# Seven operand tiles whose low halves move 128 bytes away from their high halves

## The chip, the cores and the metric

The kernel runs on one core of a Trainium2 chip. The metric is the time of one execution on the device, in microseconds (us). TensorE (PE in the profile) multiplies matrices, and its weight loads have a row of their own (PEld). VectorE (DVE), ScalarE (ACT) and GpSimd (POOL) do the elementwise work. SyncE (SP) issues every DMA. SBUF is the on-chip memory, PSUM the one that TensorE writes its sums to.

## The reference

A block-causal attention (4 batches, 8 heads, 576 positions, head size 64) gives 2304 rows of 512 values. Two layers follow, each of them two products with an elementwise function between them:

```
x = attention(q, k, v)                    # 2304 x 512
h = x @ w_in;   x = (h * cos(h)) @ w_out  # w_in 512 x 2048, w_out 2048 x 512
h = x @ w2_in;  x = relu(h)**2 @ w2_out   # the same sizes
```

All inputs and the output are float32.

## The kernel before, in words

**Precision.** A large product is computed from halves: an operand is split into a high part `hi`, rounded to the reduced type float32r that TensorE takes, and a low part `lo`, the rest. `mm3` (line 912 and on) makes three matmuls of each block: high by high, high by low, low by high.

**Stages.** Up to some 400 us the program interleaves attention with the first half (1024 of the 2048 inner columns) of the first layer. Three stages follow, and the change is about these. Stage 0 does the other half of the first layer, stage 1 one half of the second layer, stage 2 the other half. Each stage goes over the 2304 rows in five rounds, four of 512 rows and one of 256 (`ROUNDS`, in another order in each stage).

**Seven products.** In these stages `x @ w_in` is done on 2 by 2 blocks with seven block products in place of eight (`quad`; `two` for the round of 256 rows). This needs seven forms of x, which are blocks or sums of blocks: `load_quarters` makes them with four subtractions, and `x_parts` splits each into `hi` and `lo`, in one tile `x0` to `x6` of `[128, 2, 2, 256]`: two halves (`hi`, `lo`), two 128-row blocks of the inner dimension, 256 columns. There is one buffer of each tile, in the pool `x3`. A block product (`product`) is 12 matmuls `h<-x,w` of 128 by 128 weights (from a tile `w`, a form of the weight matrix) and 256 moving columns (from a tile `x0` to `x6`). In three stages these are 2304 matmuls: 3 x (4 rounds x 2 x 7 products + 1 round x 2 x 4 products) x 12.

**Keeping the forms.** Stage 1 and stage 2 need the same forms of x. `x_parts` writes the forms of the first four rounds of stage 1 to HBM (`xp_d<-x`, 24 DMAs of 512 KB), and `kept_parts` reads them back in rounds 2 to 5 of stage 2 (`x<-xp_d`, 24 DMAs). The first round of stage 2 uses what the last of stage 1 left in the tiles.

**Order.** A recording layer (`Recorder`) takes all operations, simulates their times with a table of costs and priorities, and writes out one order for all engines. `R.unit()` in `product` gives all 12 matmuls of a product one place in the priorities, so that they stand together.

**Addresses.** In the built program every `x0` to `x6` begins 320 bytes past a multiple of 512 in its partition, and its low half 2048 bytes further on, so also 320 past a multiple of 512. The weight tiles begin 384 past a multiple of 512 where they lie in the pool `wo` (first half of a round's products) and 256 past one in the pool `wa` (second half); the intermediate tiles `gh`, `gl` and `t` begin 64 past one. The two raw tiles `x` of the same pool, which stage 2 uses again for right-hand factors, begin 320 past one.

Of the kernel before, what the change touches and what calls it, by code (L numbers as in the profile page):

```python
# [2 lines left out]

# [8 lines left out]
F32R = mybir.dt.float32r  # L12
# [6 lines left out]
PSUM = bass.MemoryType.PSUM  # L19
# [37 lines left out]
class View:  # L57
    def __init__(self, vt, chain, ix, halves):
        self.vt, self.chain, self.ix, self.halves = vt, chain, ix, halves
# [34 lines left out]


class VTile(View):
    def __init__(self, pool, shape, dtype, tag, bufs, whole=False):
        self.pool, self.shape, self.dtype, self.tag, self.bufs = pool, shape, dtype, tag, bufs
        self.whole = whole
        n = int(np.prod(shape[1:]))  # L100
        self.grain = 32 if n >= 32 else 1
        self.full = (1 << (2 * (n // self.grain + 1))) - 1
        self.real = None
        self.users = []
        self.bank = self.banks = self.before = None
        super().__init__(self, [], np.arange(n).reshape(shape[1:]), 3)

    def alloc(self):
        if self.real is None:
            tag = self.tag if self.bank is None else f"bank{self.bank}"  # L110
            self.real = self.pool().tile(self.shape, self.dtype, tag=tag, name=self.tag, bufs=self.bufs)


class Banks:
# [30 lines left out]
class Recorder:  # L145
# [21 lines left out]
        self.phase = 0  # L167
        self.base = None

    def tile(self, pool, shape, dtype, tag, bufs=1, whole=False):  # L170
        return VTile(pool, shape, dtype, tag, bufs, whole)

    @contextmanager
    def of(self, kind):
# [207 lines left out]
def f(v):  # L382
    return v.bitcast(F32)


def real(v):
    return v.ap() if isinstance(v, View) else v
# [3 lines left out]
def kernel(  # L391
# [25 lines left out]
    R = Recorder()  # L417


    def of(kind):  # L420
        def wrap(fn):
            def run(*args, **kw):
                with R.of(kind):
                    return fn(*args, **kw)

            return run

        return wrap
# [40 lines left out]
    def hi_part(hi, x):  # L469
        n = hi.size  # L470
        flexible(
            "hi",
            {
                "POOL": (
                    "POOL", n * 0.836 + 160,
                    lambda: nc.gpsimd.tensor_scalar(real(hi), real(x), 1.0, 1.0, op0=ALU.mult, op1=ALU.mult),  # L476
                ),
                "DVE": (
                    "DVE", n / 1.92 + 68, lambda: nc.vector.tensor_scalar(real(hi), real(x), 1.0, None, op0=ALU.mult), 2,
                ),  # L480
                "ACT": ("ACT", n / 1.2 + 92, lambda: nc.scalar.activation(real(hi), real(x), ACTF.Copy)),  # L481
            },
            [hi], [x],
        )

    def lo_part(lo, x, hi):
        n = lo.size
        if psum(x):
            return tt(lo, x, f(hi), ALU.subtract)
        flexible(  # L490
            "lo",
            {
                "POOL": (
                    "POOL", n * 2.1 + 350,
                    lambda: nc.gpsimd.tensor_tensor(real(lo), real(x), real(f(hi)), op=ALU.subtract), 1,
                ),
                "DVE": (
                    "DVE", n / 0.96 + 68,
                    lambda: nc.vector.tensor_tensor(real(lo), real(x), real(f(hi)), op=ALU.subtract), 1,  # L499
                ),  # L500
            },
            [lo], [x, hi],
        )
# [76 lines left out]
    def dma(out, in_, size, service=None):  # L580
        R.op(
            "DMA", max(400.0, size / 360.0), lambda: nc.sync.dma_start(out=real(out), in_=real(in_)), [out], [in_],
            lat=1250,
        ).service = size / 420.0 if service is None else service
# [5 lines left out]
    class Pool:  # L590


        def __init__(self, name, **kw):
            self.name, self.kw, self.pool, self.after, self.stack = name, kw, None, (), None
# [18 lines left out]
    def later(names, **kw):  # L613
        return [Pool(n, **kw) for n in names]
# [32 lines left out]
    xs_p, tmp = opened(s1, "xs1", "tmp1")  # L647
    (sb,) = opened(att, "att", side="right")

    def T(pool, shape, dtype, tag, bufs=1):  # L650
        return R.tile(pool, shape, dtype, tag, bufs, whole=pool.kw.get("space") == PSUM)

    x_d = T(dram, [KD, 128, NT], F32, "x_d")
    y1_d = T(dram, [KD, 128, NT], F32, "y1_d")
    y_d = T(dram, [KD, 128, NT], F32, "y_d")


# [27 lines left out]
    for i in range(2):  # L685
# [3 lines left out]
        whole = T(sb, [128, 128], F32, f"whole{i}")  # L689
# [589 lines left out]
    for group, steps in WORK:  # L1279
# [6 lines left out]
        if group in ((0, 2), (1, 1)):  # L1286
            c = group[0]
            left_weights(w1_in, 2 + c, wi_d[c])
        if group in ((1, 2), (2, 1)):
            c = group[0] - 1  # L1290
            staged_weights(row_chunks(w1_out, 2 + c, 3 + c), wo_d[c:c + 1])
        if group == (3, 1):
            wo_p, x3_p = later(("wo", "x3"), side="right")
# [9 lines left out]
    def raw_rows(src, c0, n):  # L1303
# [5 lines left out]
            raw.append(t)  # L1309
        return raw  # L1310

    def x_tile(j):
        return T(x3_p, [128, 2, 2, 256], F32R, f"x{j}")

    def x_parts(forms, keep):

        ops = {}
        for j, x in forms:
            t = x_tile(j)
            hi, lo = t[:, 0], t[:, 1]  # L1320
            hi_part(hi, x)
            lo_part(lo, x, hi)
            if keep is not None:
                dma(keep[j], f(t).rearrange("p j k c -> p (j k c)"), 524288)
            ops[j] = hi, lo
        return ops

    @of("forms")
    def kept_parts(keep, which):

        ops = {}
        for j in which:
            t = x_tile(j)
            dma(f(t).rearrange("p j k c -> p (j k c)"), keep[j], 524288)
            ops[j] = t[:, 0], t[:, 1]
        return ops

    @of("forms")
    def load_plain(src, c0, keep=None):

        x1, x2 = raw_rows(src, c0, 256)
        d = T(tmp3, [128, 2, 256], F32, "t0")
        add(d, x2, x1, ALU.subtract)
        return x_parts(((0, x1), (1, x2), (4, d)), keep)

    @of("forms")
    def load_quarters(src, c0, keep=None):

        raw = raw_rows(src, c0, 512)
        b11, b12, b21, b22 = [t[:, :, o:o + 256] for t in raw for o in (0, 256)]  # L1350
        t1, t2, t3, t4 = [T(tmp3, [128, 2, 256], F32, f"t{i}") for i in range(4)]
        add(t1, b12, b11, ALU.subtract)
        add(t2, b22, t1, ALU.subtract)
        add(t3, b22, b12, ALU.subtract)
        add(t4, b21, t2, ALU.subtract)
        return x_parts(enumerate((b11, b21, b22, t4, t1, t2, t3)), keep)
# [195 lines left out]
    for stage in range(3):  # L1552
# [4 lines left out]
        for turn_, i in enumerate(ROUNDS[stage]):  # L1557
# [3 lines left out]
            if stage < 2:  # L1561
                xs = (load_quarters if i < 4 else load_plain)(src, c0, xp_d[i] if stage and turn_ < 4 else None)
                g = new_g()
            else:
                if turn_:
                    xs = kept_parts(xp_d[i], FIRST if i < 4 else (0, 1, 4))
                g = g_forms()
# [27 lines left out]
            if stage < 2 and 0 < turn_ < 3:  # L1595
                c = 2 * stage + turn_ - 1
# [62 lines left out]
```

## Time and profile before

| | us |
|---|---|
| median of 3 runs | 974.11 (973.11 to 974.89) |
| the profiled execution | 976.93 |
| its span, first to last instruction | 974.0 |
| PE busy in it | 953.0 (98%) |
| DVE, ACT, POOL busy | 695.7, 617.5, 204.0 |
| mean share of the TensorE clock granted | 0.989 |

The page gives each engine's busy time over the span. A matmul's duration in it covers the time in the pipeline, and matmuls overlap: one of 256 columns is shown with some 278 ns, while the next starts some 115 ns later. So the pace of a run of matmuls is read from the timeline, which merges a run of like instructions into one row with its start, its length and its count: the length less one duration, over the count less one, is the distance from start to start.

### The profile page before, as it was taken

The page shows a single profiled execution, that of the slowest core. Times are in us where ns is not written, and L with a number is a line of the kernel's source. Part 1 is how long each engine was busy: PE and PEld are TensorE (multiplying, and loading weights), DVE is VectorE, ACT ScalarE, POOL GpSimd, SP SyncE. Part 2 cuts the span into 40 slices and gives each one's busy share as a digit, 9 for nine tenths or more (in the row PEclk, how much of TensorE's full clock was granted, in tenths as well). Part 3 has the DMA queues.
Part 4 walks back from the last instruction along what each step waited for, and adds up shares of the span by engine and source line. Part 5 has one row for each costly group of instructions (what it writes and reads, how often), then busy time and mean ns, then how long its engine had stood idle before and what let it go on. Part 6 is the DMA issues. An engine that isn't in the chain of part 4 may idle for free.

```text
span 974.0 us, 19286 instructions
## 1 busy us (share of the span) xinstructions
PE 953.0 (98%) x6996; PEld 858.4 (88%) x6996; DVE 695.7 (71%) x1548; ACT 617.5 (63%) x1332; POOL 204.0 (21%) x299
## 2 busy tenths in 40 slices
PE   7879999999999999999999989999999999999998
PEld 5757987889897989998989879988998889999998
DVE  5998544675778455696879966997976737658565
ACT  6888688897878785574768655767664433324322
POOL 3223244588677771000000000000000000000000
PEclk8979999999999999999999999999999999999999
DMA  6754333455656449353355999897866779525321
GB/s 172 197 149 124 74 81 83 112 154 154 192 175 181 141 138 363 121 186 137 109 184 170 299 372 320 270 327 250 306 191 221 265 263 414 190 100 195 96 73 61
DMA packets 155150, 185.29 MB, mean 190 GB/s; under 512 B 71728, under 2 KB 119856, under 8 KB 155056
## 3 DMA queue, kind: packets, MB, share of 16 engines
q1 hardware_dynamic: 155056, 184.07, 57.9%
q8 instruction: 55, 0.90, 0.4%
q14 instruction: 39, 0.32, 0.1%
HBM read 114.29 MB, written 69.73 MB: 189 GB/s over the span
## 4 chain that ended last, share of the span: by engine, by line
PE 90%; DVE 5%; ACT 2%; DMA 1%; issue 1%; POOL 0%; POOLq 0%; DVEq 0%; ACTq 0%
PE y L557 39%; PE h L557 36%; PE t L575 6%; PE a L567 5%; PE s L567 4%; PE s L557 1%; DMA wi_d<-so 1%; DVE c L458 1%; DVE e L1059 1%; ACT e L442 1%; DMA x<-x_d 1%; DVE c L757 0%; DVE r L451 0%; DVE gl L499 0%; DVE w L499 0%
## 5 line engine op out<-in xcount | busy, mean ns | idle before, releaser
L557 PE MATMUL h<-x,w 128*128 128x256 f32 x2304 | 283.0, 278 | 0.2 <-ACT u L510 0.2
L557 PEld LDWEIGHTS h<-x,w 128*128 128x128 f32 x2304 | 278.3, 188 | 5.5 <-ACT u L510 0.3
L557 PE MATMUL y<-gh,w 128*128 128x256 f32 (+2 forms) x832 | 207.2, 329 | 8.2 <-POOL w L476 4.3
L557 PEld LDWEIGHTS y<-gh,w 128*128 128x128 f32 x832 | 142.8, 190 | 19.8 <-POOL w L476 4.8
L557 PE MATMUL y<-gl,w 128*128 128x256 f32 (+2 forms) x416 | 135.9, 329 | 0.0
L557 PE MATMUL y<-w,gh 128*128 128x512 f32 (+1 forms) x450 | 116.0, 353 | 0.4 <-DVE gh L499 0.4
L1059 DVE CUSTOM_DVE_ANT_0 e<-s,mask 128x288 f32<-128x288 f32 (+4 forms) x160 | 70.9, 479 | 32.8 <-PE s L567 26.2
L442 ACT ACTIVATE e<-e,st 128x256 f32<-128x256 f32 (+4 forms) x144 | 82.9, 577 | 5.9 <-DVE st L1059 3.8
L481 ACT ACTIVATE gh<-r 128x512 fp32r<-128x512 f32 (+1 forms) x101 | 58.2, 589 | 42.8 <-PE y L557 15.5
L540 POOL TENSOR_SCALAR e<-e,st 128x256 f32<-128x256 f32 (+4 forms) x120 | 73.2, 626 | 55.9 <-DVE st L1080 42.0
L557 PEld LDWEIGHTS y<-gl,w 128*128 128x128 f32 x416 | 79.1, 190 | 5.4 <-issue 0.5
L557 PEld LDWEIGHTS y<-w,gh 128*128 128x128 f32 x450 | 73.3, 188 | 11.4 <-DVE gh L499 0.6
L557 PE MATMUL y<-w,gl 128*128 128x256 f32 (+1 forms) x306 | 80.5, 332 | 0.0
L575 PE MATMUL t<-ident,e 128*128 128x128 f32 (+1 forms) x400 | 64.2, 283 | 3.8 <-DVE e L544 3.2
L557 PE MATMUL h<-xs2h,w 128*128 128x320 f32 x256 | 61.3, 313 | 0.0
L510 ACT ACTIVATE r<-t 128x384 f32<-128x384 f32 (+1 forms) x98 | 50.1, 534 | 15.2 <-PE t L575 14.5
L575 PEld LDWEIGHTS t<-ident,e 128*128 128x128 f32 (+1 forms) x400 | 46.6, 142 | 14.1 <-DVE e L544 4.7
L499 DVE TENSOR_TENSOR gl<-r,gh 128x512 fp32r<-128x512 f32 (+1 forms) x77 | 50.5, 670 | 7.8 <-ACT gh L481 7.0
L451 DVE TENSOR_TENSOR o<-y,o 128x512 f32<-128x512 f32 (+1 forms) x55 | 34.5, 634 | 27.9 <-PE y L557 26.3
L557 PEld LDWEIGHTS y<-w,gl 128*128 128x128 f32 x306 | 47.9, 188 | 6.1
L557 PE MATMUL h<-xs1h,w 128*128 128x256 f32 x256 | 51.0, 288 | 2.0 <-POOL w L476 1.1
L442 ACT ACTIVATE t<-raw,minus 128x512 int32<-128x512 int8 x64 | 48.8, 763 | 4.6 <-DMA raw<-in_moe_w_out_dram 2.6
(172 smaller groups left out, 1822.9 us busy)
## 6 DMA issues: line engine op xcount, KB each, us to landing
wi_d<-so SPq DMA_DIRECT2D x84, 256.0 KB, 3.2
w<-wi_d SPq DMA_DIRECT2D x42, 512.0 KB, 7.4
raw<-in_moe_w_in_dram SPq DMA_DIRECT2D x32, 512.0 KB, 4.8
raw<-in_moe_w_out_dram SPq DMA_DIRECT2D x32, 512.0 KB, 5.1
xp_d<-x SPq DMA_DIRECT2D x24, 512.0 KB, 6.8
x<-xp_d SPq DMA_DIRECT2D x24, 512.0 KB, 6.2
y_d<-o SPq DMA_DIRECT2D x34, 256.0 KB, 3.2
o<-y_d SPq DMA_DIRECT2D x32, 256.0 KB, 4.2
```

Of the source, the lines that this page charges most:

```text
L442: return nc.scalar.activation(real(out), real(in_), func, **kw)
L451: out.size / 0.96 + 68, lambda: nc.vector.tensor_tensor(real(out), real(a), real(b), op=op), [out], [a, b],
L458: lambda: nc.vector.scalar_tensor_tensor(real(out), real(a), s, real(b), op0=op0, op1=op1),
L481: "ACT": ("ACT", n / 1.2 + 92, lambda: nc.scalar.activation(real(hi), real(x), ACTF.Copy)),
L499: lambda: nc.vector.tensor_tensor(real(lo), real(x), real(f(hi)), op=ALU.subtract), 1,
L510: "ACT": ("ACT", n / 1.2 + 50, lambda: nc.scalar.activation(real(out), real(ps), ACTF.Copy)),
L540: lambda: nc.gpsimd.tensor_scalar(real(out), real(x), real(s), 1.0, op0=ALU.mult, op1=ALU.mult),
L557: lambda: nc.tensor.matmul(real(ps), lhsT=real(lhsT), rhs=real(rhs), start=start, stop=stop, skip_group_check=True),
L567: nc.tensor.matmul(real(ps), lhsT=real(l), rhs=real(r), start=start, stop=stop, skip_group_check=True)
L575: lambda: nc.tensor.transpose(real(out), real(in_), real(ident)[0:rows, 0:rows]), [out], [in_, ident],
L1059: lambda: nc.vector.tensor_tensor_reduce(out=real(e), in0=real(ps), in1=real(m), scale=-1.0, scalar=BIG, op0=ALU.add, op1=ALU.min, accum_o ...
```

## The change

The tiles `x0` to `x6` are allocated 32 elements (128 bytes) longer, as `[128, 1056]`, and a view on them is built whose step between the two halves is 544 elements in place of 512. The low half so begins 2176 bytes after the high half, where it began 2048 bytes after it. Within a half nothing changes. As the pool holds 7 x 128 bytes more and is filled from one fixed end, the tiles in it move too: `x3` by 128 bytes, the next by 256, and so on to `x0` and the two raw tiles `x` by 896. All of these are multiples of 128. After the change the high halves begin at 64, 192, 320 or 448 past a multiple of 512, and each low half 128 further round. The other pools stay.

The DMAs that keep the forms now have a gap on the side of SBUF, so their view there and in HBM is cut in two by halves: 2 KB runs in place of 4 KB runs, twice as many. Number, size, place and waits of the DMAs stay. No instruction of any engine moves.

```
 class VTile(View):
-    def __init__(self, pool, shape, dtype, tag, bufs, whole=False):
+    def __init__(self, pool, shape, dtype, tag, bufs, whole=False, apart=0):
...
+            if not self.apart:
+                self.real = self.pool().tile(self.shape, self.dtype, tag=tag, name=self.tag, bufs=self.bufs)
+                return
+
+            n, m = int(np.prod(self.shape[1:])), int(np.prod(self.shape[2:]))
+            t = self.pool().tile([self.shape[0], n + self.apart], self.dtype, tag=tag, name=self.tag, bufs=self.bufs)
+            a = t[:, 0:n].rearrange("p (a b c) -> p a b c", a=self.shape[1], b=self.shape[2])
+            self.real = dataclasses.replace(a, ap=[a.ap[0], [m + self.apart, self.shape[1]], *a.ap[2:]])
...
+    def by_half(t):
+        return t.rearrange("p (j c) -> p j c", j=2)
+
     def x_tile(j):
-        return T(x3_p, [128, 2, 2, 256], F32R, f"x{j}")
+        return T(x3_p, [128, 2, 2, 256], F32R, f"x{j}", 1, 32)
...
             if keep is not None:
-                dma(keep[j], f(t).rearrange("p j k c -> p (j k c)"), 524288)
+                dma(by_half(keep[j]), f(t).rearrange("p j k c -> p j (k c)"), 524288)
...
             t = x_tile(j)
-            dma(f(t).rearrange("p j k c -> p (j k c)"), keep[j], 524288)
+            dma(f(t).rearrange("p j k c -> p j (k c)"), by_half(keep[j]), 524288)
```

On SP's queue, the seven loads ahead of the second round of stage 2 stand like this in the kernel before (`xp_d` is the copy in HBM, the last column the shape of the transfer):

```order
L582 DMA x_10656<-xp_d_7857 128x1024
L582 DMA x_10667<-xp_d_7840 128x1024
L582 DMA x_10673<-xp_d_7600 128x1024
L582 DMA x_10686<-xp_d_7876 128x1024
L582 DMA x_10704<-xp_d_7617 128x1024
L582 DMA x_10721<-xp_d_7610 128x1024
L582 DMA x_10741<-xp_d_7814 128x1024
```

And like this in the changed one, at the same place of the queue:

```order
L590 DMA x_10656<-xp_d_7857 128x2x512
L590 DMA x_10667<-xp_d_7840 128x2x512
L590 DMA x_10673<-xp_d_7600 128x2x512
L590 DMA x_10686<-xp_d_7876 128x2x512
L590 DMA x_10704<-xp_d_7617 128x2x512
L590 DMA x_10721<-xp_d_7610 128x2x512
L590 DMA x_10741<-xp_d_7814 128x2x512
```

Their order is the same, and only the shape differs.

## Rows read from the trace of the kernel before

**Rows 1.** The page's first part: engine, busy us, share, instructions.

```profile
PE 953.0 (98%) x6996; PEld 858.4 (88%) x6996; DVE 695.7 (71%) x1548; ACT 617.5 (63%) x1332; POOL 204.0 (21%) x299
```

**Rows 2.** The page's chain that ended last, share of the span by engine.

```profile
PE 90%; DVE 5%; ACT 2%; DMA 1%; issue 1%; POOL 0%; POOLq 0%; DVEq 0%; ACTq 0%
```

**Rows 3.** Waits of PE from 400 us on: us in total, times, longest.

```profile
PE y L557 <- ACT gh L481: 2.7, 1, 2.7
PE y L557 <- DVE gh L499: 0.4, 1, 0.4
PE h L557 <- ACT u L510: 0.2, 1, 0.2
```

**Rows 4.** The page's costliest group: busy us, mean ns of one.

```profile
L557 PE MATMUL h<-x,w 128*128 128x256 f32 x2304 | 283.0, 278 | 0.2 <-ACT u L510 0.2
```

**Rows 5.** Timeline of PE, 793 to 811 us: start, length, engine, names, count.

```profile
792.81 14.33 PE L557 MATMUL h<-x,w 128*128 128x256 f32 x125
806.98 0.28 PE L557 MATMUL y<-raw,ws 128*128 128x256 f32 x1
807.10 4.17 PE L557 MATMUL h<-x,w 128*128 128x256 f32 x34
```

**Rows 6.** Tile h by stretches: length, busy PE, PEld, DVE, ACT, PEclk, DMA.

```profile
793.00:806.00 13.00, 13.00 (x117) 13.00 (x116) 2.76 (x4) 2.99 (x5) 1.00 0.89 318
838.00:849.00 11.00, 11.00 (x96) 11.00 (x94) 2.73 (x4) 2.40 (x4) 1.00 0.59 185
```

**Rows 7.** Groups of PE, 793 to 806 us, then 838 to 848 us.

```profile
L557 PE MATMUL h<-x,w 128*128 128x256 f32 x117 | 13.4, 276 | 0.0
...
L557 PE MATMUL h<-x,w 128*128 128x256 f32 x87 | 10.4, 280 | 0.0
```

**Rows 8.** Timeline of PE, 821 to 850 us.

```profile
822.47 1.57 PE L557 MATMUL h<-x,w 128*128 128x256 f32 x12
...
824.58 0.84 PE L557 MATMUL y<-w,gl 128*128 128x256 f32 x6
825.27 1.57 PE L557 MATMUL h<-x,w 128*128 128x256 f32 x12
...
837.12 0.84 PE L557 MATMUL y<-w,gh 128*128 128x256 f32 x6
837.80 11.47 PE L557 MATMUL h<-x,w 128*128 128x256 f32 x96
```

**Rows 9.** Timeline of PE, 597 to 600 us.

```profile
597.96 0.28 PE L557 MATMUL y<-gl,w 128*128 128x256 f32 x1
598.07 0.28 PE L557 MATMUL y<-gh,w 128*128 128x256 f32 x1
598.18 1.07 PE L557 MATMUL h<-x,w 128*128 128x256 f32 x8
```

**Rows 10.** Timeline of PE, 812 to 818.5 us.

```profile
816.17 0.88 PE L557 MATMUL y<-x,t 128*128 128x256 f32 x6
816.89 0.88 PE L557 MATMUL y<-x,gl 128*128 128x256 f32 x6
```

**Rows 11.** DMA issues: names, count, KB each, median us from issue to landing.

```profile
xp_d<-x SPq DMA_DIRECT2D x24, 512.0 KB, 6.8
x<-xp_d SPq DMA_DIRECT2D x24, 512.0 KB, 6.2
...
x<-x_d SPq DMA_DIRECT2D x8, 512.0 KB, 4.5
x<-y_d SPq DMA_DIRECT2D x8, 512.0 KB, 5.8
```

**Rows 12.** SP's issues of tile x: 812.0 to 812.4 us, then 812 to 820 us.

```profile
L582 SPq DMA_DIRECT2D x<-xp_d x1: 320/320/320, 812.1 to 812.1; - x1
DMA to landing us min/median/max: 9.9/9.9/9.9
...
L582 SPq DMA_DIRECT2D x<-xp_d x7: 319/319/320, 812.1 to 819.5; - x7
```

More of the change, by code (lines that the diff above doesn't have):

```diff
@@ L1 @@
+import dataclasses
 import heapq
@@ L96 @@
 class VTile(View):
-    def __init__(self, pool, shape, dtype, tag, bufs, whole=False):
+    def __init__(self, pool, shape, dtype, tag, bufs, whole=False, apart=0):
         self.pool, self.shape, self.dtype, self.tag, self.bufs = pool, shape, dtype, tag, bufs
-        self.whole = whole
+        self.whole, self.apart = whole, apart
         n = int(np.prod(shape[1:]))
@@ L110, in alloc @@
             tag = self.tag if self.bank is None else f"bank{self.bank}"
-            self.real = self.pool().tile(self.shape, self.dtype, tag=tag, name=self.tag, bufs=self.bufs)
+            if not self.apart:
[5 more added lines that the diff above has]
+            self.real = dataclasses.replace(a, ap=[a.ap[0], [m + self.apart, self.shape[1]], *a.ap[2:]])
 class Banks:
@@ L168, in __init__, with tile @@
         self.base = None
-    def tile(self, pool, shape, dtype, tag, bufs=1, whole=False):
-        return VTile(pool, shape, dtype, tag, bufs, whole)
+    def tile(self, pool, shape, dtype, tag, bufs=1, whole=False, apart=0):
+        return VTile(pool, shape, dtype, tag, bufs, whole, apart)
     @contextmanager
@@ L648, with T @@
     (sb,) = opened(att, "att", side="right")
-    def T(pool, shape, dtype, tag, bufs=1):
-        return R.tile(pool, shape, dtype, tag, bufs, whole=pool.kw.get("space") == PSUM)
+    def T(pool, shape, dtype, tag, bufs=1, apart=0):
+        return R.tile(pool, shape, dtype, tag, bufs, pool.kw.get("space") == PSUM, apart)
     x_d = T(dram, [KD, 128, NT], F32, "x_d")
```

## The prediction

> **What bounds the kernel now.** I read the page's first part and its chain first. PE is busy for 953.0 of 974.0 us [rows 1], and of the chain that ended last 90% is PE [rows 2]. Then the waits of PE from 400 us on, where the three stages that use the tiles lie: there are three waits, 3.3 us in all, and none ends with a DMA [rows 3]. The reader is to see in these that from 400 us on the time is the sum of the matmuls' distances from start to start. A change there counts only if it alters that distance, or makes a wait that isn't there now.
>
> Next I read the distance. The group that the change touches is `h<-x,w`, 2304 matmuls [rows 4]. The timeline shows two paces of it. From 792.81 us 125 of them take 14.33 us: less the last one's 0.28 that is 14.05 over 124 distances, 113.3 ns [rows 5]. From 837.80 us 96 take 11.47: 11.19 over 95, 117.8 ns [rows 8]. [...] The shown duration of one goes along, 276 ns at pace A and 280 at pace B [rows 7]. Over all 2304 the mean is 278 [rows 4], midway: about 1152 go at pace B. All at A would be 1152 x 4.5 ns = 5.2 us less than now, all at B 5.2 us more. There is a third pace in the trace, C: six `y<-x,gl` take 0.88 us, (0.88 - 0.28) / 5 = 120 ns [rows 10].
>
> **The change part by part.** It removes and adds no instruction and moves none. It changes addresses, and the shape of 48 DMAs.
>
> *Matmuls.* A third of the 2304, the 768 that stream a low half, now start 128 bytes further round in a cycle of 512 than those before and behind them; with the high halves these tiles move as a whole too, each by its own multiple of 128. What is that worth? The trace has no low half at another offset, so I look for places where an address takes such a step.
>
> - The weights take one. The stretch of 125 runs through the end of the first half of its round (weights at 384 past a multiple of 512) into the second half (256 past one), where the four last products of the run, 48 matmuls, lie. Were these at pace B, the mean would be (77 x 113.3 + 48 x 117.8) / 125 = 115.0 ns; it is 113.3 [rows 5]. The 96 at pace B cross the same step after 24 [rows 8].
> - The moving operand takes one, of 256 bytes. Up to 598.07 us `y<-gh,w` streams tiles at 64 past a multiple of 512, from 598.18 us on `h<-x,w` streams `x0` at 320. The starts are 597.96, 598.07 and 598.18: 110 ns apart to the row's resolution of 10, and the eight that follow take (1.07 - 0.28) / 7 = 113 ns [rows 9]. No step is seen.
> - The same addresses run at both paces. `x2` and `x3` with weights at 384 stand in the stretch at A (the last two products before the weights change) and again at the head of the one at B, a round later [rows 5, 8]. What differs is what ran before: the stretches at B follow `y` products. Behind the one `y<-raw,ws` at 806.98 us the pace is (4.17 - 0.28) / 33 = 117.9 ns, where it was 113.3 up to it [rows 5].
>
> So a pace is taken up at a switch between kinds of products and kept, and a step of 128 or 256 bytes in one of the operands changes neither. The places with C have moving operands and weights that both lie at an odd multiple of 64, while `h<-x,w` has the one at an odd, the other at an even multiple [rows 10, 5]. The change moves by multiples of 128, so it leaves odd odd. I therefore take 0 for the matmuls. Bounds, from the paces seen: -5.2 us (none left at B) and, at 120 ns for all 2304, 2304 x 120 - 2304 x (113.3 + 117.8) / 2 = +10.3 us.
>
> [...]
>
> *The 48 DMAs.* Each keeps its 512 KB and its place and is cut into twice as many runs of 2 KB. There are 512 KB loads in 2 KB runs already, `x<-x_d` and `x<-y_d`, with a median of 4.5 and 5.8 us to landing, against 6.2 and 6.8 of the 48 [rows 11]: shorter runs aren't seen to be slower, though these run beside other traffic. The cover is PE's own work, and it is thinnest ahead of the second round of stage 2. The seven loads there are issued from 812.1 to 819.5 us, 1.23 us apart, and the first lands 9.9 us after its issue, at 822.0 [rows 12]; the first matmul that needs it starts at 822.47 [rows 8]. That is some 0.5 us of slack; the second load (issued at about 813.4, landed by about 823.4) is needed at 825.27 [rows 8], 1.9 us of slack, and those behind it have more. Below, the cost is 0. Above, if every transfer took twice its 1.23 us, the first would come 1.23 - 0.5 = 0.7 us late and the second 2.5 - 1.9 = 0.6, which is the same wait and not another: 0.7 us once. I take 0, since the nearest rows are no slower. The 24 stores of stage 1 have nobody on PE behind them [rows 3].
>
> *Elementwise work* on the forms (ACT and DVE in stages 0 and 1) has the same instructions at other addresses; PE waits 0.2 us for ACT in all `h` products and not at all for DVE there [rows 3], which is the cover. If it were gone, a wait on ACT or DVE would stand ahead of `h` in the waits.
>
> **The sum.** Matmuls 0, DMAs 0, elementwise 0. The profiled execution took 976.93 us, span 974.0 and 2.9 around it, and stays there; the median of the runs, 974.11, lies 2.8 under it, and I forecast for the median 974.1 + 0 = 974.1. As paces are taken up at switches, a different moment of a few waits may hand out some anew: the rows show stretches of 12, 34, 96 and 125. With 38 matmuls in one, an estimate, there are some 60; if half of them changed, each by 38 x 4.5 ns = 0.17 us in either direction, that would be about 0.17 x square root of 30 = 0.9 us. This is within 1.95 us, the 0.2% that a measurement of this kernel can tell from no change.
>
> **Rivals.**
>
> *Faster: pace B needs the halves aligned.* A low half that no longer lies where the high half lies in the cycle of 512 would push a stretch at B out of its pattern, since two streams that met in each matmul no longer meet in the low ones. For it: one cause seems shared by all stretches at B, as they have the same distance of 117.8 ns in products of different tiles [rows 5, 8]. Against it: the weights' step of 128 bytes doesn't do that. Price: -5.2 us if all go, -2.6 if half go; 968.9 to 971.5, about 970.
>
> *Slower: pace A needs them.* Now each matmul's operand ends where, in the cycle of 512, the next one's begins, high or low; with the change the cycle jumps by 128 at the start of each low half and back behind it, 1536 jumps in the 2304. If fetching ahead across the jump costs what a switch costs, the stretches at A fall to B: 1152 x 4.5 = +5.2 us, 979.3; at 120 ns for all of them 984.4. For it: behind switches, where such jumps are, pace A is lost [rows 5, 8]. Against: at 598 us a jump of the moving operand isn't followed by a loss [rows 9]. It decides from one jump in three being paid for on: 512 x 4.5 = 2.3 us.
>
> *The change doesn't do what it says* is excluded for the addresses, which stand in the built program; that it does nothing to the time is the forecast itself. A wait on the first load (at most 0.7 us) lies within no change too.
>
> **How the numbers follow.** Forecast 0.62: the three steps without effect are the only direct evidence, but none is of a low half. Faster rival 0.21, slower 0.17: their prices are equal, and the pattern of B, kept only from a switch on, looks the easier one to break. Forecast's own range 972.5 to 975.8. The range to 8 in 10 leaves out a tenth on each side: half of the faster rival's 0.21 lies under 970, and half of the slower's 0.17 over 978, so 970 to 978. Faster by over 0.2% 0.21, within 0.62, slower 0.17.
>
> **What would show it.** Right: 276 to 280 ns with a mean near 278 for the 2304, 125 at A in one row near 793 us and 96 at B near 838 us, no DMA in the waits of PE. Faster: the stretch at 838 us at 113 ns, mean near 276. Slower: the stretch at 793 us at 118 ns or more, mean 280 or over. The step on the DMAs is wrong if `h` waits for `x<-xp_d` at 822 us by over 0.7 us. The forecast is wrong if the mean distance of `h<-x,w` moves by over 0.9 ns (2304 x 0.85 ns = 1.95 us).

## The result, and the profile after

The changed kernel takes 979.35 us (median of 6 runs, 978.46 to 981.2), the kernel before, on the same chip, 974.5 (973.09 to 976.18): ratio 1.0053, 95% interval 1.0037 to 1.0070, so 4.85 us slower. I had forecast 974.1. The price is that of the rival *Slower: pace A needs them*, 979.3.

The first part of the page of the changed kernel, then its row of the touched group (line 565 was 557):

```profile
PE 957.4 (98%) x6996; PEld 862.4 (88%) x6996; DVE 697.1 (71%) x1548; ACT 617.1 (63%) x1332; POOL 204.2 (21%) x299
```

```profile
L565 PE MATMUL h<-x,w 128*128 128x256 f32 x2304 | 287.7, 280 | 0.0
```

PE is busy 4.4 us longer than in [rows 1], with the same number of instructions; DVE and ACT differ by less than 1.5. The group `h<-x,w` is busy 287.7 us where it was 283.0 [rows 4]: 4.7 us, all that is to be explained. Divided by 2304 that is 2.0 ns more from one start to the next, and the mean shown duration, 278 before, is now the 280 of pace B, the one of 117.8 ns [rows 7, 8].

The waits of PE from 400 us on:

```profile
PE y L565 <- ACT gh L489: 0.8, 2, 0.5
PE y L565 <- DVE gh L507: 0.4, 1, 0.4
```

They come to 1.2 us, 2.1 less than in [rows 3]. So the two spans differ by only 4.7 - 2.1 = 2.6 us (976.6 and 974.0): the profiled execution of before holds one wait of 2.7 us for `gh`, and lies 2.4 us over the median of its own runs. No wait is on a DMA. The 48 transfers (names, KB, median us to landing) are 0.2 us quicker than in [rows 11]:

```profile
xp_d<-x SPq DMA_DIRECT2D x24, 512.0 KB, 6.6
x<-xp_d SPq DMA_DIRECT2D x24, 512.0 KB, 6.0
```

The timeline of PE where before the stretch of 125 stood at pace A, 113.3 ns [rows 5]:

```profile
793.53 15.67 PE L565 MATMUL h<-x,w 128*128 128x256 f32 x132
809.04 0.28 PE L565 MATMUL y<-raw,ws 128*128 128x256 f32 x1
809.16 3.11 PE L565 MATMUL h<-x,w 128*128 128x256 f32 x25
```

(15.67 - 0.28) / 131 = 117.5 ns, where it was 113.3. Tile h in two stretches of the changed kernel, as in [rows 6] (length, busy PE with count, granted clock, DMA):

```profile
794.00:807.00 13.00, 13.00 (x113) 1.00 0.92 323
840.20:851.20 11.00, 11.00 (x96) 1.00 0.56 169
```

In the first, 13 us now hold 113 matmuls, not 117; in the second 11 us hold 96 as they did. The granted clock is 1.00 in both, as it was in both of [rows 6], and PE is busy throughout: neither the clock nor a wait makes the difference. So what was at pace A lost it, and what was at pace B stayed. From the start times of all neighbours in the group (2201 distances in each trace, gaps left out) the mean goes from 115.6 to 117.6 ns, and 175 distances lie under 115 ns where 1107 did. The rest are no longer even: 112 to 123 ns, about a mean near that of B.

### The profile page after: what moved, and what is told of

Same layout as the page of the kernel before. It is cut to its first block, busy times and chain, and to the rows that moved or that the text cites. A ratio compares the mean times of both kernels' runs of the same rounds, so it can differ in the third digit from the quotient of the medians.

```text
span 976.6 us, 19286 instructions
## 1 busy us (share of the span) xinstructions
PE 957.4 (98%) x6996; PEld 862.4 (88%) x6996; DVE 697.1 (71%) x1548; ACT 617.1 (63%) x1332; POOL 204.2 (21%) x299
## 4 chain that ended last, share of the span: by engine, by line
PE 90%; DVE 4%; DMA 3%; ACT 2%; POOL 1%; issue 1%; SPq 0%; POOLq 0%; ACTq 0%; DVEq 0%
PE y L565 38%; PE h L565 37%; PE t L583 6%; PE a L575 5%; PE s L575 3%; DMA wi_d<-so 2%; PE s L565 1%; DMA raw<-in_moe_w_in_dram 1%; DVE c L466 1%; DVE c L765 0%; POOL e L548 0%; DVE e L1067 0%; ACT e L450 0%; DVE gl L507 0%; DVE r L459 0%
## 5 line engine op out<-in xcount | busy, mean ns | idle before, releaser
L565 PE MATMUL h<-x,w 128*128 128x256 f32 x2304 | 287.7, 280 | 0.0
L565 PEld LDWEIGHTS h<-x,w 128*128 128x128 f32 x2304 | 282.8, 188 | 5.3 <-ACT u L518 0.2
L565 PE MATMUL y<-w,gh 128*128 128x512 f32 (+1 forms) x450 | 116.1, 353 | 0.4 <-DVE gh L507 0.4
```

The source lines that it names most:

```text
L565: lambda: nc.tensor.matmul(real(ps), lhsT=real(lhsT), rhs=real(rhs), start=start, stop=stop, skip_group_check=True),
```

## The experiments

A remark on the rows: a window of 10 us counts the matmuls that reach into it, so its pace is (10.00 + 0.28) / count: 91 or 90 at pace A, 87 or 88 at B, 85 or 86 at C. "Mean distance" is worked out as above from the start times of the group.

**Jumps, own addresses, or the DMAs?** Three kernels put the seven forms into one block of SBUF, all high halves, a gap, all low halves, so that each address can be chosen; order and transfers stay, and a few waits of DVE are met one matmul earlier.

```diff
-            self.real = self.pool().tile(self.shape, self.dtype, tag=tag, name=self.tag, bufs=self.bufs)
...
+            h, l = HALVES[self.tag]
+            block = self.pool.block = self.pool.block or self.pool().tile([128, BLOCK], self.dtype, tag="block", ...)
+            a = block[:, h:h + 1024].rearrange("p (a b c) -> p a b c", a=2, b=2)
+            self.real = dataclasses.replace(a, ap=[a.ap[0], [l - h, 2], *a.ap[2:]])
```

`HALVES` gives the places of the two halves in 4-byte elements: `x0` stands at (0, 3712) for the gap of 512 bytes, (0, 3616) for 128, (0, 3648) for 256, and each further form 512 elements on.

> The kernel before with the seven x forms in one block of SBUF: all high halves in a row, then 512 bytes of nothing, then all low halves. Every half begins at 320 modulo 512, as in the kernel before; the form's DMAs go in two runs of 2 KB, as in the changed kernel. Theory 1 (pace A needs each 256-column matmul's moving operand to begin where the one before ended, modulo 512): no jump is left, so 974.5 us and the mean distance of the 2304 matmuls near 115.6 ns. Rival 2 (the forms' own start addresses modulo 512 decide): the same, 974.5. Rival 3 (the 2 KB runs of the DMAs cost the time): 979. Rival 4 (chance: any change of addresses draws the paces anew): anything from 970 to 979.

> The same block, but the low halves 128 bytes past a multiple of 512 behind the high ones: high halves all at 320 modulo 512, as before, low halves all at 448. Theory 1: 1536 of the 2304 matmuls begin 128 bytes away from where the one before ended, as in the changed kernel: 979.3 us, mean distance near 117.8 ns. Rival 2 (own addresses): only the 768 matmuls on low halves have a new address, a third of 5 us: 976. Rival 3 (2 KB runs): 979, as for the 512-byte gap. Rival 4: anything from 970 to 979.

> The same block with the low halves 256 bytes past a multiple of 512: high halves at 320 modulo 512, low halves at 64. Theory 1 with a period of 512 bytes: 1536 jumps again, 979. Theory 1 with a period of 256 bytes: no jump counts, 974.5. Rival 2: a third of the effect at most, 976. Rival 3: 979. Rival 4: anything from 970 to 979.

The fourth keeps the changed kernel's tiles but puts the low half directly behind the high one (32 elements of extra length, no gap, no offset), and its DMAs go in one run again:

```diff
...
-        return T(x3_p, [128, 2, 2, 256], F32R, f"x{j}", 1, 32)
+        return T(x3_p, [128, 2, 2, 256], F32R, f"x{j}", 1, (32, 0, 0))
...
```

> The seven forms' tiles are 128 bytes longer, as in the changed kernel, so each begins where it does there (64, 192, 320 or 448 modulo 512), but the low half follows the high half directly and the DMAs are one run of 4 KB, as before. Theory 1: no jump inside a product; only some 190 places where the form changes have one: if each costs only its own matmul, +0.4 us, 975; if a jump leaves pace A for the rest of its product of 12 matmuls, up to 979. Rival 2 (own addresses): 1944 of the 2304 matmuls have another address, 978.7. Rival 3 (2 KB runs): 974.5. Rival 4: anything from 970 to 979.

The group of h in the four, in the order gap 512, 128, 256, then tiles moved:

```profile
L569 PE MATMUL h<-block,w 128*128 128x256 f32 x2304 | 283.0, 278 | 0.2 <-ACT u L522 0.2
```

```profile
L569 PE MATMUL h<-block,w 128*128 128x256 f32 x2304 | 287.9, 280 | 1.8 <-ACT u L522 1.8
```

```profile
L569 PE MATMUL h<-block,w 128*128 128x256 f32 x2304 | 283.3, 278 | 0.8 <-ACT u L522 0.8
```

```profile
L566 PE MATMUL h<-x,w 128*128 128x256 f32 x2304 | 285.7, 279 | 0.0
```

| kernel | ratio to before (95%) | mean distance |
|---|---|---|
| gap 512 | 1.0001 (0.9990 to 1.0012) | 115.6 ns |
| gap 128 | 1.0040 (1.0022 to 1.0059) | 117.7 ns |
| gap 256 | 1.0000 (0.9987 to 1.0014) | 115.6 ns |
| tiles moved, no gap | 1.0025 (1.0013 to 1.0037) | 116.8 ns |

The gap of 512 has the changed kernel's DMA runs of 2 KB and costs nothing: rival 3 falls. The gap of 256 costs nothing either, and both repeat the paces of before nearly one by one (1108 and 1100 distances under 115 ns; 1107 before): rival 4, chance, falls, and 256 bytes count as no jump, so the cycle is 256 bytes and not 512. The gap of 128, with every high half where it was, brings the whole 4.9 us back in the group: rival 2 had a third. The moved tiles have no jump inside a product and only 95 jumps of 128 modulo 256 between products, and cost 2.7 us in the group. That is far more than 95 matmuls' worth: a jump's effect outlasts its own matmul. Lay the built program's addresses beside the start times of this trace, and the pace before and behind most of these jumps can be told. Where the distance from stationary to moving operand goes from 192 to 64 modulo 256, the pace is B behind it in 23 cases of 23, 15 of which came from A; where it goes from 64 to 192, it is A in 20 cases of the 26 that came from B, and B in all 4 that came from A. In 30 of the 95 the weights step by 128 together with the moving operand, so that the distance stays; there too A is lost, in all 6 cases that came from it. So a jump of the moving operand that meets pace A ends it whichever way the distance goes, and only a step of the distance from 64 to 192 mostly turns B to A.

**Fewer jumps at the same addresses.** Each product runs its eight matmuls on the high half first:

```diff
-                    mm3(ps[:, m], (w[i][:, 0, c], w[i][:, 1, c]), (hi[:, k], lo[:, k]), ...)
+                    for n in range(2):
+                        matmul(ps[:, m], w[i][:, n, c], hi[:, k], ...)
+            for m in range(2):
+                for k in range(2):
+                    ...
+                    matmul(ps[:, m], w[i][:, 0, c], lo[:, k], False, k == 1, holds)
```

> Control for the next kernel: forms as in the block with the 512-byte gap (no jump), but each product of 12 matmuls runs its eight matmuls on the high half first and its four on the low half last, where it was high, low, high by turns. The list of instructions comes out somewhat differently for this, so its time against the kernel before is open, 972 to 978; it is to be compared with the next one.

> The same order (eight matmuls on the high half, then four on the low half), the low halves 128 bytes past a multiple of 512: the same addresses as in the block with the 128-byte gap, which ran at 980.1, and the same share of matmuls on them, but only two jumps in 12 matmuls, 384 in all instead of 1536. Theory 1 (a jump between consecutive moving operands is what costs, and the pace comes back after it): a quarter to a half of 5 us above its control. Rival 2 (a low half 128 bytes off costs wherever it stands): the full 5 us above its control. Rival 5 (any jump throws the pace to B until the next gap): also nearly the full 5 us.

The order costs both a wait of 6.4 us on `w` elsewhere, so only the two are compared: 987.45 and 990.37 us, ratios 1.0126 (1.0108 to 1.0144) and 1.0150 (1.0133 to 1.0168). These intervals overlap, so the reading rests on the group rows, control first:

```profile
L569 PE MATMUL h<-block,w 128*128 128x256 f32 x2304 | 282.6, 278 | 2.7 <-DVE r L463 1.4
```

```profile
L569 PE MATMUL h<-block,w 128*128 128x256 f32 x2304 | 285.6, 280 | 0.7 <-ACT block L493 0.5
```

302 jumps (some of the 384 fall where other matmuls stand between) cost 3.0 us in the group, 1517 (gap 128) cost 4.9, 95 (tiles moved) cost 2.7. So my "a quarter to a half" of 5 us was too low and rival 5, nearly all of it, too high. The price grows far less than the count of jumps. An estimate of its bound is what was at pace A: 1107 distances, at 4.5 ns each 5.0 us.

**The place against the stationary operand.** The block 64 bytes on (both operands at even multiples of 64); everything 64 bytes on (moving even, stationary odd); jumps of 64:

```diff
-    shim(ctx, "shim1", 32)
+    shim(ctx, "shim1", 96)
-    shim(ctx, "shim3", 96, side="right")
+    shim(ctx, "shim3", 160, side="right")
```

That is the second. The others change only the block's table: `x0` at (16, 3728) for the first, (0, 3600) for the third.

> The block with the 512-byte gap, moved as a whole by 64 bytes: no jump inside or between products (all halves at 384 modulo 512), but the moving operands now begin at even multiples of 64, as the stationary ones do (256 and 384). Theory 1 with period 256 alone (only jumps count, the place does not): 975. Theory 6 (the place counts against the stationary operand's: both on even or both on odd multiples of 64 give pace C, as the trace of before has it for the matmuls of y on x and gl): all 2304 at 120 ns, (120 - 115.6) x 2304 = +10 us, 985.

> The kernel before with every tile of SBUF moved by 64 bytes (upwards on the left side, downwards on the right), nothing else: the forms begin at 256 modulo 512 and the weights of h at 320, which is how the matmuls of y on w and gh stand in the kernel before (256 and 64), and those always run at pace A there; y's own matmuls then stand as h's did. Theory 1 (only jumps count): 975. Theory 6 (place against the stationary operand): h all at pace A, (115.6 - 113.3) x 2304 = 5.3 us less, 970, from which y's 256-column matmuls may take back up to 2 us.

> One look: the block with the low halves 64 bytes past a multiple of 512 (high halves at 320 modulo 512, low halves at 384): 1536 jumps of 64 bytes, and the 768 matmuls on low halves stand on an even multiple of 64 as their weights do. Theory 1: at least as slow as the 128-byte gap, mean distance 117.7 ns or more, 980; with theory 6, 768 of them at 120 ns and more, up to 118.5 ns and 982. If a jump of 64 bytes counted for nothing: 115.6 ns, 975.

Group rows in that order:

```profile
L569 PE MATMUL h<-block,w 128*128 128x256 f32 x2304 | 290.8, 282 | 0.0
```

```profile
L557 PE MATMUL h<-x,w 128*128 128x256 f32 x2304 | 283.8, 279 | 0.7 <-DMA x<-xp_d 0.6
```

```profile
L569 PE MATMUL h<-block,w 128*128 128x256 f32 x2304 | 289.2, 281 | 0.1
```

With both on even multiples the ratio is 1.0069 (1.0056 to 1.0081), the mean distance 119.1 ns, and 1114 of the distances are 120: pace C, without one jump, as the prediction read it from [rows 10]; the expectation had 10 us by theory 6, and 7.8 came in the group. The 64-byte jumps (a single run, 980.32 us) cost 6.2 us in the group. The other half of theory 6 fell: with all places exchanged h was at B as often as before or a little more (1005 distances under 115 ns, mean 115.7), ratio 1.0015 (1.0005 to 1.0025). Its premise was not right either: the matmuls `y<-w,gh` of before don't always run at A, 107 of 148 of their distances lie under 115 ns.

**By itself.** Stretches of 96 matmuls on zeros in one accumulator, without waits, put in ahead of the kernel. Three kernels do this, and each ran once. The code is that of the second and third; the first steps only the moving operand:

```diff
...
+            for mov, stat, lo, wl in PARTS:
+                for i in range(96):
+                    o, w = mov + (lo if i % 3 == 1 else 0), stat + (wl if i % 3 == 2 else 0)
+                    nc.tensor.matmul(real(ps)[:, 0:256], lhsT=real(z)[:, w:w + 128], rhs=real(z)[:, o:o + 256], ...)
```

> The disputed cost by itself: the kernel before with nine stretches of 96 matmuls of 256 columns on zeros put in at its start, back to back in one accumulator, no waits between, the stationary operand always the same. In a stretch the middle one of each three reads its moving operand 0, 128, 256 or 512 bytes further on; the place is as h has it (moving on an odd multiple of 64, stationary on an even one), but for one stretch with both on odd ones. In order: 0, 0, 128, 0, 256, 128, 512, both odd 0, 0. The time of the whole kernel (about 100 us more) says nothing. Theory 1 with period 256: the two stretches with 128 at 117.5 ns and more from start to start; those with 0, 256 and 512 alike, at 113.3 or 117.8 as they fall; both odd: 120. Against it: all stretches alike, which would mean that the offset matters only beside changing weights and accumulators.

Windows of PE inside the stretches with steps of 128, 256, 128, then with both operands on odd multiples, then without steps:

```profile
32.00:42.00 10.00, 10.00 (x88) 1.00 0.36 119
...
54.50:64.50 10.00, 10.00 (x88) 1.00 0.31 109
65.50:75.50 10.00, 10.00 (x87) 1.00 0.01 2
...
88.00:98.00 10.00, 10.00 (x85) 1.00 0.00 0
100.00:110.00 10.00, 10.00 (x87) 1.00 0.01 2
```

All stand at B, 117.8 ns, jumps or none, and at 120 where both are odd. The four stretches not shown are at 117.8 too, by their start times. Jumps of 128 don't slow pace B on average (117.79 with them, 117.77 without). So they can cost only by what they do to pace A, and this run never had it.

> The separate measurement again, with ten stretches of 96 matmuls, to see what brings pace A about: without a jump the last such run stayed at 117.77 ns throughout, and in the kernel with h on even multiples pace B turned to pace A wherever the stationary operand's address stepped from 192 to 64 modulo 256. Now the third of each three reads its stationary operand 0, 128 or 256 bytes further on, the middle one its moving operand 0 or 128. Moving on odd and stationary on even multiples of 64: steps of the stationary operand 0, 128, 0; moving on even and stationary on odd ones: 0, 128, 0; then both operands with steps of 128, in either place; then a stationary step of 256 (odd moving); then none (even moving). Theory 7 (a 128-byte step of the stationary operand sets pace A, a 128-byte step of the moving one unsets it): the stretches with stationary steps alone at 113.3 ns, and those after them without steps stay at 113.3; with both steps 117.8. Theory 1 alone (only the moving operand's steps count, and they only keep pace A away): all stretches near 117.8.

Windows in the first, second and sixth stretch, then those with both operands stepping (two places), then the stationary step of 256:

```profile
9.00:19.00 10.00, 10.00 (x91) 1.00 0.58 168
20.00:30.00 10.00, 10.00 (x91) 1.00 0.52 159
...
64.00:74.00 10.00, 10.00 (x91) 1.00 0.01 2
75.00:85.00 10.00, 10.00 (x85) 1.00 0.00 0
86.00:96.00 10.00, 10.00 (x87) 1.00 0.00 0
97.50:107.50 10.00, 10.00 (x90) 1.00 0.01 2
```

This time the first stretch was at A already, with the same instructions and addresses as the first of the run before. So these alone don't set the pace. At the entry the two differ: the first two starts are 207 ns apart here and 200 in the run at B. Whether that decides isn't shown. Steps of the stationary operand by 128 leave A alone, as the prediction had read from [rows 5]; the moving operand's, with them, end it (120.8 ns in the first of the two places, 117.7 in the second). Whether stationary steps set A this run can't say.

> The separate measurement a third time, twelve stretches of 96 matmuls, since no stretch so far had steps of the moving operand alone and began at pace A. Moving on odd, stationary on even multiples of 64 and always the same. Steps of the middle moving operand in order: 0; 256; 0; then all 96 of a stretch 128 further on (one single step at its start); back again (one single step); 128 in every third; 0; then the stretch with both operands stepping by 128 on the other multiples, to shake the pace; 0; one single step of 128; 128 in every third; 0. Theory 1 (jumps of 128 keep pace A away): wherever pace A, 113.3 ns, is found, the stretch with 128 in every third leaves it for 117.8 on average or more, and the one without steps behind it stays at 117.8 or finds A again by chance; a step of 256 keeps A. A single step of 128: either A is lost for the whole stretch behind it (a jump throws the pace to B), or a few matmuls are slower and A comes back (a jump costs only its own matmuls). Against theory 1: 113.3 in the stretches with 128 in every third.

Windows in the stretches four to seven (all 128 on; back; 128 in every third; none), then nine to twelve (none; 128 on; 128 in every third; none):

```profile
43.00:53.00 10.00, 10.00 (x88) 1.00 0.50 176
54.50:64.50 10.00, 10.00 (x91) 1.00 0.32 108
65.50:75.50 10.00, 10.00 (x87) 1.00 0.01 2
76.50:86.50 10.00, 10.00 (x90) 1.00 0.00 0
...
99.00:109.00 10.00, 10.00 (x91) 1.00 0.01 2
110.00:120.00 10.00, 10.00 (x87) 1.00 0.01 2
121.00:131.00 10.00, 10.00 (x88) 1.00 0.00 0
132.00:142.00 10.00, 10.00 (x87) 1.00 0.00 0
```

The fifth stretch is at A, the sixth, with jumps of the moving operand alone, isn't; the seventh, without, is again. One single step of 128 behind the ninth puts the tenth to B for all of its 96, and it was one single step back that had put the fifth to A. No stretch in which jumps of 128 of the moving operand come again and again is at A, in any of the three runs; where they stop, the pace may be either.

**Can pace A be had?** Three tries, each with the order, semaphores and transfers of before. The first stands h's moving operand on even, its weights on odd multiples of 64 throughout, and leaves y as it is:

```diff
-            self.real = self.pool().tile(self.shape, self.dtype, tag=tag, name=self.tag, bufs=self.bufs)
...
+            o = 16 * (SLOTS[self.pool.slot] % 2 != self.odd)
...
+            t = self.pool().tile([128, 1040], self.dtype, ...)[:, o:o + 1024]
```

> An attempt at a faster kernel, from the traces so far: no jumps, and all 2304 matmuls of h with the moving operand at an even multiple of 64 bytes (256 modulo 512) and the stationary one at an odd multiple, as the matmuls of y on w stand in the kernel before and keep standing here. For this the wo and x3 pools lie 64 bytes lower, and the tiles of the wa pool are 64 bytes longer, with h's weights on odd and y's weights on even multiples. Order, waits and transfers are those of before. Theory 6 (place against the stationary operand decides between the paces): h at pace A but for the first few of each stretch, 2304 x (115.6 - 113.6) = 4.6 us less, 970.4; in the run with every tile moved by 64 bytes half of h stayed at B, so half of it, 972.5, is the other end. Theory 1 alone (only jumps count): 975.

```profile
L569 PE MATMUL h<-x,w 128*128 128x256 f32 x2304 | 282.7, 278 | 0.0
```

973.15 us, ratio 0.9984 (0.9973 to 0.9995): a little under the kernel before, but not by its reason. The group gained 0.3 us of the 4.6 expected; where the rest of the 1.6 us comes from isn't shown. The second exchanges the places of the two pools of weights:

> The kernel before with its pools moved by multiples of 128 bytes: the wa pool and all behind it 128 up, wo 128 down and the forms 256 down, so that the forms stay at 64 modulo 128 and at one place, and only the order of the two weight places is turned round: weights of h at 256 modulo 512 in the first half of each round and at 384 in the second, where it was 384 and then 256; the matmuls of y stand as before against their weights modulo 256. Order, waits, transfers as before. Theory 8 (pace B turns to pace A where the distance from the stationary to the moving operand steps from 64 to 192 modulo 256, as in the separate measurement where the moving operand went 128 back, and in the kernel with h on even multiples; the opposite step leaves the pace): the second half of each round, 1152 matmuls of which some 610 were at B, goes to A, 610 x 4.5 ns = 2.7 us less, 971.9 to 972.2, mean distance 114.4 ns. Against it (which pace a stretch takes is settled at its start and differs from layout to layout without a rule): 115.6 ns and 974 to 976 again, or anything between 113.5 and 117.8 with the time to match.

```diff
-    shim(ctx, "shim1", 32)
+    shim(ctx, "shim1", 160)
-                if i:
-                    shim(stack, "shim4", 64, side="right")
+                if old == (sb,):
+                    shim(stack, f"shim{4 + i}", (128, 192)[i], side="right")
...
```

The group up to the step in the middle of the round near 801 us, and from there on (duration minimum, median, maximum):

```profile
L557 PE MATMUL h<-x,w x82: 277/279/280, 791.9 to 801.4; 128*128 128x256 f32 x82
```

```profile
L557 PE MATMUL h<-x,w x50: 276/276/280, 801.4 to 807.0; 128*128 128x256 f32 x50
```

The step does turn B (279 ns) to A (276), in 11 cases of the 13 that came from B. But the first halves, at A before [rows 5], are at B in exchange: of the distances under 115 ns, 339 are in first halves and 646 in second ones, where it was 718 and 389. The whole group is busy 283.5 us, and the ratio is 1.0010 (1.0000 to 1.0021).

The third makes the weight tiles of the first halves 128 bytes longer:

> An attempt at a faster kernel: the seven weight tiles of the wo pool, which serve the first half of each round of h, are 128 bytes longer, so that the stationary operand stands at 0 or at 128 modulo 256 by turns of products, with the moving one at 64 throughout as before; the wa pool and the forms' places modulo 512 stay. Order, waits and transfers are those of before. Some 50 steps of the distance from stationary to moving operand from 64 to 192 modulo 256 come about by this, all by the stationary operand, and as many back. Theory 8 (a step from 64 to 192 turns B to A, the step back by the stationary operand leaves A): of the 1152 matmuls of the first halves nearly all from the first such step on at A, 370 that were not, x 4.5 ns = 1.7 us less, and the second halves that follow without a break begin at A too, where stage 2 was at B, 4 x 72 x 4.5 ns = 1.3 us less: 971 to 973, mean distance 114.3. Against it (the steps hand out paces as before, some better and some worse): 115.6 ns and 974 to 976.

```diff
...
+            t = self.pool().tile([128, 1056], self.dtype, ...)[:, 0:1024]
+            self.real = t.rearrange("p (a b) -> p a b", a=2)
...
```

```profile
L562 PE MATMUL h<-x,w 128*128 128x256 f32 x2304 | 282.8, 278 | 0.9 <-DMA x<-xp_d 0.9
```

The steps from 64 to 192 turned B to A in 13 cases of 15, and the mean distance is 115.4 ns, but y's 256-column matmuls, 116.1 ns before, came to 116.6, and `h` waits 0.9 us for `x<-xp_d`, which it did not before. The ratio is 0.9997 (0.9986 to 1.0008). The effect of a step is mostly as theory 8 has it, but there is no gain. The likely reason is that the `y` products between the stretches hand out the paces anew; no run isolates that.

## Why the prediction was wrong

**The bound** was read rightly: from 400 us on the time is the sum of the distances, and 4.7 of the 4.85 us are in them.

**The matmuls** are the step that failed: "So a pace is taken up at a switch between kinds of products and kept, and a step of 128 or 256 bytes in one of the operands changes neither. [...] I therefore take 0 for the matmuls." The first half of it stands in part: the separate stretches keep a pace for 96 matmuls. The second half was drawn from two kinds of steps, and both were harmless ones. The 128 bytes were the stationary operand's from the first half of a round to the second (384 to 256 past a multiple of 512), which left the pace in all 20 cases of that trace that can be told. The moving operand's step was 256 bytes, and these cost nothing (gap 256: 115.6 ns, as before). From these two I took a third, 128 bytes of the moving operand and repeated, as seen, and it is the one that costs: 4.7 us in the group, against 0.

The trace of before had a counterexample that I did not look for: the stationary operand's step the other way, 256 to 384. In one run of 36 `h<-x,w` without a break the weights take it at 519.15 us. The timeline's row of the run, then its matmuls up to there and from there on (duration minimum, median, maximum):

```profile
516.80 4.33 PE L557 MATMUL h<-x,w 128*128 128x256 f32 x36
```

```profile
L557 PE MATMUL h<-x,w x20: 278/280/281, 516.8 to 519.0; 128*128 128x256 f32 x20
L557 PE MATMUL h<-x,w x16: 276/276/277, 519.1 to 520.9; 128*128 128x256 f32 x16
```

The pace turns from B to A there, as it does at 4 of the 6 such steps of this trace that come from B. So "changes neither" was wrong even for the operand on which it was seen, and so was the point against the faster rival, that the weights' step doesn't push a stretch out of B.

The bounds held it, and the rival had it: the stretches at A fall to B, 1152 x 4.5 = 5.2 us, 979.3. The matmuls lost 4.7, and 175 distances still lie under 115 ns. What it named as the cause, a jump of the moving operand that ends pace A, was right but for the cycle, which is 256 bytes and not 512; its "against", the jump at 598 us, was one of 256 and so none. That its price came out to the microsecond is in part luck: it has every matmul of A go to an even B, and the runs show an uneven pace with about that mean. Whether fetching ahead is behind it, as the rival guessed, no run shows, nor whether two streams meet in a matmul, as the faster rival had it. I gave it 0.17, less than the faster rival, because B, "kept only from a switch on", looked easier to break. It is the other way: jumps leave the mean of B at 117.8 (m_jump) and end A (in the changed kernel 175 distances under 115 ns where 1107 were; e_move, all 25 cases that came from A; m_step, 87 matmuls in a window after 91).

**The odd and even multiples of 64** were right as far as the change went: it leaves them, and where they are made equal pace C comes (s_even: 1114 distances of 120 ns).

**The rivals** looked for the cause in the addresses, rightly, and had 0.38 together. The runs show paces of 113.3, 117.8 and 120 ns that depend, among other things, on where the streaming operand lies against its forerunner (gap 128 and gap 256: 117.7 and 115.6 ns in the mean) and against the weights (s_even: 119.1).

**The DMAs** at 0 were right: no wait on them, and the 2 KB runs alone (gap 512) cost 0.01%, within its interval. **Elementwise work** at 0 was right: the waits of h on ACT are gone rather than grown.

**Range and chances.** 979.35 lies 1.35 us past the range's upper end of 978; half of the slower rival's 0.17 was left beyond it.

## What to carry to other kernels

Where PE is the bound and one shape of matmul makes up most of it, work out its distance from start to start, not its mean duration alone: two levels a few per cent apart in one kernel, at one clock (here 113.3 and 117.8 ns at 1.00), are a reason to look at the addresses. Before padding or moving tiles, try first what cost nothing here: the moving operands of matmuls that run one after the other equal modulo 256 bytes (a gap of 256 had the ratio 1.0000, one of 128 1.0040), and moving and stationary operand not both on odd or both on even multiples of 64 (both on even: s_even, 1.0069). In this kernel that is worth 0.4 to 0.7%, some 4 to 7 us of 975 (gap 128, the change itself, s_even). An observation that "a step does nothing" holds for the operand and the size it was made on.

## What the runs showed of the hardware

For 256-column float32r matmuls at a granted clock of 1.00, back to back without waits, three even paces were seen: 113.3 ns [rows 5], 117.8 [rows 8] and 120 (s_even). Bfloat16 matmuls of 256 columns on zeros at the start of the kernel before follow each other faster:

```profile
7.61 0.49 PE L557 MATMUL h<-zeros 128*128 128x256 bf16 x3
```

(0.49 - 0.27) / 2 = 0.11 us, 109 or 110 ns by the start times, at a granted clock of 1.00. Both their operands begin at the same odd multiple of 64, the place that costs float32r matmuls 120 ns (m_jump). So what is said here of places is shown for float32r alone.

113.3 and 117.8 both last at the same addresses, over 96 matmuls in the separate runs (the first stretch of m_flip, 91 in a window of 10 us, and of m_jump, at 117.8). One 128-byte step of the moving operand turned A to B for the whole of the next 96 matmuls, and one step back turned B to A (m_step: 91 and then 87 matmuls in a window of 10 us; 88 and then 91); in e_move every such step that met A ended it (15, 4 and 6 cases), and of those that met B, mostly the ones that took the distance from stationary to moving operand from 64 to 192 modulo 256 turned it to A (20 of 26). A step of the stationary operand that takes this distance from 64 to 192 turns B to A in 24 of 28 cases (e_cross, e_alt), but in only 4 of 6 in the kernel before and 4 of 7 in e_move, and the opposite one leaves the pace in 40 of 43. Why it is so, and what makes the first matmul of a stretch take the one or the other, was not settled.
